# A two-layer attention and convolution kernel: the stage between the two, with its first loads, last softmax sums, interleaving and row normalisation rearranged

## The chip, the cores and the metric

The kernel runs on one core of one Trainium2 chip. The metric is the device time of one execution in microseconds, the median of three runs. The engines are named as in the profile: PE (TensorE, matrix products and transposes), PEld (its weight loads), DVE (VectorE), ACT (ScalarE), POOL (GpSimd) and SP (SyncE, which here only issues DMAs). Each engine executes its own instructions in program order and waits at an instruction until what it needs is there, so whatever stands behind a waiting instruction waits too.

## What is computed

`x` has 2048 rows of 640 numbers. Four blocks follow each other, each on the LayerNorm of the rows and added to `x`: attention (32 heads of 20), a long convolution, attention again, the convolution again, with the same weights.

```python
x = x + _A_ref(_layernorm(x), wqkv, wo)    # softmax(q k^T / sqrt(20)) v, then @ wo
x = x + _B_ref(_layernorm(x), ...)         # y = irfft(rfft(u) * rfft(K)) + u * D_skip
x = x + _A_ref(_layernorm(x), wqkv, wo)
x = x + _B_ref(_layernorm(x), ...)
# K[d, l] = 2 Re sum_n C[d, n] dt[d] exp(A[d, n] dt[d] l), 640 x 2048, the same in both layers
```

## The kernel before the change

**Attention.** The 32 heads are taken in eight groups of four, and each group in four blocks of 512 queries: 32 blocks, one after the other. For each block PE makes scores `S` (L866), ACT exponentiates them into `pt` (L869), and PE multiplies `pt` with the values into two accumulators `pa` (L900). One extra column of the values holds ones, so row 20 of each head's accumulator is the sum that its softmax divides by. At the end of a block (L903 to L950) DVE adds the two accumulators into `oc`. The sums then take a way through DRAM: POOL writes them out (`sums`, `dn<-oc`), reads them back spread over 128 partitions (`load`, `dr<-dn`), DVE inverts them (`invert`), POOL writes them (`back`, `dn<-dr`) and reads them back repeated for each row of a head (`spread`, `db<-dn`), and DVE multiplies (`scale`, `oc<-oc,db`). In the first layer `scale` waits in a list until the next block's accumulators have been emptied. POOL then stores `oc` to `ot` in DRAM (`store_block`). The second layer has another way for its last block only, `at_once` (L882): a 128 by 128 selector matrix `dsel` is multiplied with `oc`, which repeats the sums over the rows of their heads in one product `m<-oc,dsel`, and DVE clamps, inverts and multiplies.

**Between attention and convolution** (`out_proj`, L1310). For each of the 16 row tiles, `ot` is loaded (`otl`), split into a rounded part `oh` and a rest `ol`, and multiplied with `wo` in 30 products `po` of 320 columns (10 with `ol`, then 20 with `oh`). DVE adds the two results to `x` and takes the row statistics. When two row tiles are done, `ln` (L1660, `ln_u` at L1214) normalises both: a chain of small DVE operations with one ACT square root ends in `nb`, then ACT writes `u` and its rounding `uh` for each of the two, and POOL (DVE for the last row tile) the rest `ul`.

In the first layer this stage also transforms the convolution kernel `K` (`ktransform`, L1237). Its work is cut into 70 steps, and each step issues its own transposes or products and the copies that empty them: `by_time` (transposes `pkt<-kl`, copies `ktrh` on ACT and `ktrl` on DVE), `first_stage` (24 products `pkx`, copies `kx`), `turned` (transposes `pkt<-kx`, copies `kxt`) and `ends` (32 small products `pkf`, copies `kn`, stored as `kha` and `khb`). Steps and products share PE: after every eighth product `po` one step is issued (`weave(1)`, L1333), and what is left of the steps follows behind the last product (`weave(1000)`, L1366). The transforms' PSUM tiles come from the pool `X`, which has two buffers.

The first channel block of `K` is read into `kl` (`load_kl`, L1210). In the first layer this is issued on SP among other loads when the last attention block begins (`rest` in `prefetch`, L1181): three parts of `x`, then `skip`, `f2`, then `kl`. Before its transposes DVE adds one column to it (`kl<-kl,skip`, L1246).

**Convolution** (`ssm`, L1382). Five channel blocks of 128 run through a software pipeline of 55 turns (L1505). `stage1` makes products `psx` from `uh` and `ul`, which ACT and DVE empty into the two halves of `x1`; `stage2a` transposes (`pst`, emptied by ACT into `xt`); `sets` makes further products, `product` multiplies with the transformed kernel on DVE (shuffle `t`, `ka`) and POOL (`kb`, `ka`), and `stage3` and `stage4` transform back (`psv`, `psy`). All eight parts of `stage1` for channel block 0 come ahead of the pipeline (L1499); those of block 1 go one into each of its first eight turns, beside that turn's `pst`. Both use the pool `X`, but for parts 2, 3, 6 and 7 of block 0, which use the pool `M` (two buffers).

## Time and profile before

| | us |
|---|---|
| median of three runs | 2674.0 |
| the three runs | 2670.18, 2674.0, 2676.64 |
| the profiled execution, its own time | 2673.58 |
| its span, first to last instruction | 2671.8 |
| PE busy, ACT busy, DVE busy, POOL busy | 2496.7, 2344.9, 1510.4, 817.3 |
| first layer, end of the last attention product to the end of the last `po` | 1091.8 to 1259.6 |
| first layer, first `pst` of the convolution | 1283.7 |
| second layer, first `pst` of the convolution | 2527.7 |

All times within the execution are microseconds from the start of the span. A row of the timeline gives start, duration, engine, source line, operation, what is written and read with its shape, a count, and in brackets how long the engine sat idle before it and what ended that idle time. Nearly every DVE and ACT row has line 78, a helper that records the operations, so they are told apart by their tiles. A table of stretches gives, for each stretch, the busy time of each engine with the number of instructions, and the granted clock of PE as a share of full speed.

### The profile page before, as it was taken

How to read it: one execution, taken by the hardware profiler on the slowest of the kernel's cores; microseconds unless marked ns; L12 is line 12 of the kernel's file. 1: busy time of each engine (PE TensorE's matmuls, PEld its weight loads, DVE VectorE, ACT ScalarE, POOL GpSimd, SP SyncE). 2: the span in 40 equal slices, each digit the busy share in tenths (PEclk: the TensorE clock that was granted, in tenths of full speed). 3: DMA queues.
4: the chain of work that ended last, by engine and by line, in shares of the span. 5: the costliest groups of instructions: out<-in, count | busy, mean ns of one | idle time of the engine just before them, and what ended most of it. 6: DMA issues, size and time to landing. Idle time of an engine off the chain costs nothing.

```text
span 2671.8 us, 118793 instructions
## 1 busy us (share of the span) xinstructions
PE 2496.7 (93%) x52386; PEld 1412.8 (53%) x52386; DVE 1510.4 (57%) x3407; ACT 2344.9 (88%) x2763; POOL 817.3 (31%) x1250
## 2 busy tenths in 40 slices
PE   7899999999999988798898999999999998999898
PEld 3445444444444433587796444454444443444798
DVE  8687778778855884376787333231233221154775
ACT  7899999999999999555765799999999999999474
POOL 1123334233332423311581122222222222222285
PEclk9999999999999999899999999999999999999899
DMA  6523222222221222553652121121121113222366
GB/s 208 184 52 86 61 77 71 74 63 69 65 53 48 61 58 75 185 187 150 230 174 70 43 57 51 51 59 46 43 66 38 54 29 93 69 66 56 129 192 182
DMA packets 186446, 242.21 MB, mean 91 GB/s; under 512 B 43616, under 2 KB 128832, under 8 KB 184256
## 3 DMA queue, kind: packets, MB, share of 16 engines
q1 hardware_dynamic: 149904, 188.22, 22.2%
q0 software_dynamic: 36016, 46.30, 7.2%
q8 instruction: 413, 6.77, 1.0%
q14 instruction: 113, 0.93, 0.1%
HBM read 158.37 MB, written 76.01 MB: 88 GB/s over the span
## 4 chain that ended last, share of the span: by engine, by line
ACT 57%; PE 19%; issue 13%; DMA 5%; DVE 4%; POOL 1%; SPq 0%; ACTq 0%; POOLq 0%; DVEq 0%
ACT pt L78 54%; PE psy L1412 3%; PE psv L1412 2%; PE pa L900 2%; PE psx L1412 2%; PE po L193 2%; PE S L866 2%; PE pst L1433 1%; DMA kl<-kd 1%; DVE x L78 1%; PE pkt L196 1%; PE pq L771 1%; PE m L618 1%; DMA qop<-qs 1%; PE pkx L193 1%
## 5 line engine op out<-in xcount | busy, mean ns | idle before, releaser
L78 ACT ACTIVATE pt<-S 128x1024 f32<-128x1024 f32 x2048 | 1927.7, 1033 | 32.5 <-PE S L866 20.3
L900 PE MATMUL pa<-pt,V 64*32 64x512 f32 x16384 | 1094.4, 590 | 0.2 <-DVE oc L78 0.2
L866 PE MATMUL S<-qop,kop 61*32 61x512 f16 x16384 | 873.6, 381 | 86.5 <-ACT pt L78 67.7
L866 PEld LDWEIGHTS <-kop 61*32 61x32 f16 x16384 | 365.4, 89 | 740.3 <-issue 624.4
L900 PEld LDWEIGHTS pa<-pt,V 64*32 64x32 f32 x16384 | 311.9, 106 | 68.7 <-issue 7.9
L78 POOL DMA_DIRECT2D dn<-oc x252 | 124.0, 499 | 591.4 <-DVE oc L78 573.2
L78 DVE TENSOR_SCALAR qc<-m 128x512 f32<-128x512 f32 (+1 forms) x68 | 46.8, 688 | 282.7 <-PE m L618 282.7
L78 POOL DMA_DIRECT2D db<-dn x252 | 126.9, 510 | 139.0 <-DMA dn<-dr 136.1
L78 POOL DMA_DIRECT2D ot<-oc x256 | 130.1, 516 | 81.6 <-DVE oc L78 52.0
L78 DVE COPY oc<-pa 128x512 f32<-128x512 f32 x64 | 44.2, 691 | 194.3 <-PE pa L900 183.4
L618 PE MATMUL m<-xh,wh 64*32 64x512 f16 x2560 | 144.2, 378 | 2.9 <-DVE qc L78 2.9
L618 PE MATMUL m<-xh,wl 64*32 64x512 f16 x2560 | 143.8, 376 | 0.0
L618 PE MATMUL m<-xl,wh 64*32 64x512 f16 x2560 | 143.1, 376 | 0.0
L78 ACT COPY xt<-pst 128x1024 f16<-128x1024 f16 x80 | 81.2, 1015 | 59.7 <-PE pst L1433 59.7
L618 PEld LDWEIGHTS <-wh 64*32 64x32 f16 x5120 | 90.1, 93 | 76.5 <-issue 34.8
L78 POOL DMA_DIRECT2D dn<-dr x63 | 35.0, 555 | 304.9 <-DVE dr L78 289.8
L1461 POOL TENSOR_TENSOR kb<-t,kb 128x512 f32<-128x512 f32 x76 | 97.1, 1278 | 84.8 <-DVE t L78 46.0
L78 DVE TENSOR_SCALAR V<-m 128x160 f32<-128x160 f32 x64 | 20.7, 324 | 161.3 <-PE m L584 161.3
L78 DVE TENSOR_TENSOR kb<-ktab 128x512 f32<-128x512 f32 x160 | 106.3, 683 | 0.0
L584 PEld LDWEIGHTS <-xh 128*128 128x128 f16 x960 | 79.5, 98 | 44.8 <-issue 28.9
L335 PEld LDWEIGHTS m<-kb,ka 128*32 128x32 f32 x3840 | 61.2, 110 | 74.8 <-issue 56.4
L1461 POOL TENSOR_TENSOR ka<-ka,kb 128x512 f32<-128x512 f32 x76 | 97.4, 1281 | 6.0
(312 smaller groups left out, 3944.2 us busy)
## 6 DMA issues: line engine op xcount, KB each, us to landing
ka<-kha SPq DMA_DIRECT2D x80, 256.0 KB
kb<-khb SPq DMA_DIRECT2D x80, 256.0 KB
db<-dn POOLq DMA_DIRECT2D x252, 64.0 KB, 3.2
kop<-ks SPq DMA_DIRECT2D x176, 80.0 KB
kpw<-wd POOLq DMA_DIRECT2D x60, 192.0 KB, 4.6
qop<-qs SPq DMA_DIRECT2D x256, 40.0 KB
ot<-oc POOLq DMA_DIRECT2D x256, 40.0 KB, 2.8
kha<-kn SPq DMA_DIRECT2D x20, 512.0 KB
```

The costliest lines, as they stand in the source:

```text
L78: made = f(out, *a, **k)
L193: chain(te.matmul(*a, **k))
L196: chain(te.transpose(*a, **k))
L335: chain(te.matmul(ps[32 * j:32 * j + 32, c8, :], a[n][:, ch, :], b[n][:, dd, :], start=(n == 0), stop=(n == 2), tile_position=(0, 32 * j)))
L584: chain(te.matmul(ps[:, :n], a_[:, ct, sl], m[:, ct, :], start=(k == 0), stop=(k == 14)))
L618: chain(te.matmul(ps[r][32 * t:32 * t + 32, :], a_[rows, ct, 32 * u:32 * u + 32], m[rows, ct, 512 * v:512 * v + 512], start=(k == 0), stop ...
L771: te.matmul(pq, a_[:, ct, :], m[:, ct, sl], start=(n == 0), stop=(n == 14))
L866: chain(te.matmul(S[32 * t:32 * t + 32, 512 * r:512 * r + 512], kt_[rows, kc + 32 * t:kc + 32 * t + 32], qt[rows, :], start=True, stop=Tru ...
L900: chain(te.matmul(pa[r][32 * j:32 * j + 32, :], V[rows, kt, VP * h:VP * h + 32], pts[j // 2][rows, 512 * (j % 2):512 * (j % 2) + 512], sta ...
L1412: at("pe", te.matmul(*a, **k))
L1433: at("pe", te.transpose(pt[:, k, g, :], of_group(x1[k], 4 * q + g), id16))
L1461: at("pool", getattr(ge, f)(*a))
```

## The change

It has six parts.

1. In `prefetch` the small loads and `kl` are put ahead of the second to fourth part of `x`, and a selector `dsel` for the first layer (`late[0]`) is loaded with them. The addition `kl<-kl,skip` of block 0 is tied behind the DVE instruction that was last issued when turn 12 of the last attention block was written (`late[1]`).
2. The last block of the first layer takes the way `at_once`, as that of the second layer does.
3. One step of `ktransform` is issued ahead of the first product `po`, and then one after every seventh product instead of every eighth.
4. `ln` makes the statistics of a pair at once, as before, but the writing of `u`, `uh` and `ul` is a piece for each row tile, and after each row tile's products one piece is issued. This holds in both layers.
5. `stage1` of channel block 1 takes its PSUM tiles from `M` for parts 1, 3 and 5, in both layers.
6. `stage1` of channel block 0 takes all its tiles from `X` in the second layer; in the first it keeps `M` for parts 2, 3, 6 and 7.

```diff
--- before.py
+++ after.py
@@ -883,7 +883,7 @@
 
             pb = pst("M", [P, 512], F32, tag="m0", name="m0")
             db = ev.tile([P, 512], F32, bufs=1, name="db")
-            te.matmul(pb, dsel[0], oc, start=True, stop=True)
+            te.matmul(pb, (dsel or late)[0], oc, start=True, stop=True)
             ve.tensor_scalar_max(db, pb, 1e-30)
             ve.reciprocal(db, db)
             ve.tensor_mul(oc, oc, db)
@@ -912,7 +912,7 @@
                 sums_[0] = plan.dve + 0.15
                 while scaled:
                     scaled.pop(0)()
-                if dsel and blk == NBK - 1:
+                if blk == NBK - 1:
                     later.append((plan.dve, lambda: at_once(oc, blk)))
                     return
 
@@ -1125,6 +1125,8 @@
                             load_k(g, j, 1)
                         if g2 == g and qb2:
                             load_q(g, j, qb2, n + 1)
+                if kt == 12 and first_layer and n == len(turns) - 1:
+                    late.append(ve.last)
                 if kt == 8 and g2 != g:
                     need(NEED[g2])
                     for j in range(2):
@@ -1174,11 +1176,13 @@
                       w1.tile([P, 2, 32], F32, name="f2"), w1.tile([P, 4, NI // 2, 4, 32], F32, name="kx1"),
                       *(w1.tile([P, NI, P], F16, name=f"ktr{n}") for n in "hl"),
                       *(w1.tile([P, 4, 4, P], F32, name=f"kxt{n}") for n in range(2))]
+            late[:] = [w1.tile([P, P], F32, name="dsel")]
 
             def small():
                 sy.dma_start(kl0[1], dsk)
+                sy.dma_start(late[0], c_dn)
                 sy.dma_start(kl0[2], c_f2.rearrange("p (s m) -> p s m", s=2))
-            rest.extend((small, lambda: load_kl(0)))
+            rest[1:1] = small, lambda: load_kl(0)
             with tc.tile_pool(name="wos", bufs=NCT, side="right") as ws:
                 for ct in range(NCT):
                     wt = ws.tile([P, D], F32, name="wot")
@@ -1205,7 +1209,7 @@
             weights(ct)
         rest.extend(lambda ct=ct: halves(ct) for ct in range(NCT))
         return x, c, woh, wol, w2
-    ups, kl0 = [], []
+    ups, kl0, late = [], [], []
 
     def load_kl(b):
 
@@ -1243,7 +1247,7 @@
         def by_time(b, h):
 
             if h == 0:
-                ve.tensor_add(kl[:, 0:1], kl[:, 0:1], skip[:, b:b + 1])
+                tie(ve.tensor_add(kl[:, 0:1], kl[:, 0:1], skip[:, b:b + 1]), None if b else late[1])
             klv = kl.rearrange("d (p i) -> d i p", i=NI)
             for i4 in (2 * h, 2 * h + 1):
                 pt = pst("X", [P, 4, P], F32, tag="X", name="pkt")
@@ -1329,8 +1333,9 @@
                 return
             matmul(*a, **k)
             many[0] += 1
-            if many[0] % 8 == 0:
+            if many[0] % 7 == 0:
                 weave(1)
+        weave(1)
         to_come = {s: 0 for s in range(NI)}
         for s, c0, c1 in rows.left + [e[0] for e in rows.loaded + first]:
             to_come[s] += 1
@@ -1353,16 +1358,16 @@
                 load()
                 load = None
             if due:
-                ln(*due.pop(0))
+                due.pop(0)()
             if not to_come[s]:
                 if s >= NI - LG or s % LG and s - 1 in whole:
-                    due.append((s, 1))
+                    due.extend(ln(s, 1))
                 elif s % LG == LG - 1:
-                    due.append((s + 1 - LG, LG))
+                    due.extend(ln(s + 1 - LG, LG))
             if due and len(whole) == 0:
-                ln(*due.pop(0))
+                due.pop(0)()
         while due:
-            ln(*due.pop(0))
+            due.pop(0)()
         weave(1000)
 
     def ssm_consts(c):
@@ -1415,7 +1420,8 @@
 
             def stage1(b, x1, i2):
                 bs = slice(b * P, b * P + P)
-                pool, tag = ("X", "X") if b or i2 % 4 < 2 else ("M", "mm")
+                spare = b == 1 and i2 in (1, 3, 5) or not b and i2 % 4 > 1 and not last
+                pool, tag = ("M", "mm") if spare else ("X", "X")
                 ps = pst(pool, [P, 2, 2, P], F32, tag=tag, name="psx1")
                 for i in range(2):
                     s = 2 * i2 + i
@@ -1658,10 +1664,18 @@
                     up2 = c2.enter_context(tc.tile_pool(name="up2", bufs=2 + n))
 
                     def ln(i0, m):
-                        ln_u(x, i0, m, ln_stats(lambda i: x[:, i0 + i, :], m), uh, ul, up2, not general)
+                        held = []
+
+                        def one(i):
+                            if not held:
+                                held.extend(ln_stats(lambda i: x[:, i0 + i, :], m))
+                            mv, rs = held
+                            ln_u(x, i0 + i, 1, (mv[:, i:i + 1, :], rs[:, i:i + 1]), uh, ul, up2, not general)
+                        return [lambda i=i: one(i) for i in range(m)]
                     if general:
                         for i0 in range(0, NI, LG):
-                            ln(i0, LG)
+                            for f in ln(i0, LG):
+                                f()
                     else:
                         if n == 0:
                             filler[:] = ktransform(consts[0]), 0.0, False
```

Three places show what this does to the order of instructions. The first is the start of the first layer's `out_proj`. On DVE before the change, from the addition to `kl` on (`dr` are the sums of the last block but one, `pa` the accumulators of the last block, and the multiplication with `db` is that of the last block but one):

```order
L78 TENSOR_TENSOR kl<-kl,skip 128x1
L78 TENSOR_SCALAR dr<-dr 128x16
L78 RECIPROCAL dr<-dr 128x16
L78 CAST oh<-otl 128x640
L78 TENSOR_TENSOR ol<-otl,oh 128x640
L78 COPY oc<-pa_25900 128x512
L78 TENSOR_TENSOR oc<-oc,pa_25901 128x512
L78 TENSOR_TENSOR oc<-oc,db 128x512
L78 SCALAR_TENSOR_TENSOR ktrl<-pkt,ksc,ktrh 128x512
L78 TENSOR_TENSOR ol<-otl,oh 128x640
L78 SCALAR_TENSOR_TENSOR ktrl<-pkt,ksc,ktrh 128x512 x2
```

After the change, DVE at the same place, from the end of the first row tile's split on (`m` is the product with `dsel`):

```order
L78 TENSOR_TENSOR ol<-otl,oh 128x640
L78 TENSOR_TENSOR kl<-kl,skip 128x1
L78 COPY oc<-pa_25901 128x512
L78 TENSOR_TENSOR oc<-oc,pa_25902 128x512
L78 TENSOR_TENSOR oc<-oc,db 128x512
L78 SCALAR_TENSOR_TENSOR ktrl<-pkt,ksc,ktrh 128x512
L78 TENSOR_SCALAR db<-m_26437 128x512
L78 SCALAR_TENSOR_TENSOR ktrl<-pkt,ksc,ktrh 128x512
L78 RECIPROCAL db<-db 128x512
L78 TENSOR_TENSOR ol<-otl,oh 128x640
L78 TENSOR_TENSOR oc<-oc,db 128x512
L78 SCALAR_TENSOR_TENSOR ktrl<-pkt,ksc,ktrh 128x512 x2
```

The addition now stands behind the inversion of `dr` and the first split, of which only the last row is shown, and the last block's own inversion, of 512 columns, stands between the second and the third `ktrl`. On PE, the same place before and after, from the last attention product on:

```order
L900 MATMUL pa_25901<-pt,V_93 32x512 x4
L193 MATMUL po<-woh,ol 128x320 x8
L196 MATMUL pkt<-ident,kl 128x128 x8
L193 MATMUL po<-woh,ol 128x320 x2
L193 MATMUL po<-woh,oh 128x320
L193 MATMUL po<-wol,oh 128x320
L193 MATMUL po<-woh,oh 128x320
```

```order
L900 MATMUL pa_25902<-pt,V_93 32x512 x4
L196 MATMUL pkt<-ident,kl 128x128 x8
L886 MATMUL m_26437<-oc,dsel 128x512
L193 MATMUL po<-woh,ol 128x320 x7
L196 MATMUL pkt<-ident,kl 128x128 x8
L193 MATMUL po<-woh,ol 128x320 x3
L193 MATMUL po<-woh,oh 128x320
L193 MATMUL po<-wol,oh 128x320
L193 MATMUL po<-woh,oh 128x320
```

Eight transposes and the product with `dsel` now stand ahead of the first `po`.

The second place is ACT in the same stage, at the third pair of row tiles (`lt` is the square root). Before:

```order
L78 CAST oh<-otl 128x640
L78 ACTIVATE ktrh<-pkt,ksc 128x512
L78 ACTIVATE lt<-va 128x2
L78 ACTIVATE ktrh<-pkt,ksc 128x512
L78 COPY kn_27343<-pkf_27324 128x512
L78 ACTIVATE u<-x,nb,rs 128x640 x2
L78 CAST uh<-u 128x640 x2
L78 COPY kn_27347<-pkf_27326 128x512
```

After:

```order
L78 ACTIVATE kxt_25870<-pkt,ksc 128x512
L78 ACTIVATE lt<-va 128x2
L78 ACTIVATE ktrh<-pkt,ksc 128x512
L78 ACTIVATE u<-x,nb,rs 128x640
L78 ACTIVATE ktrh<-pkt,ksc 128x512
L78 CAST uh<-u 128x640
L78 ACTIVATE u<-x,nb,rs 128x640
L78 COPY kn_27436<-pkf_27417 128x512
L78 CAST uh<-u 128x640
L78 COPY kn_27440<-pkf_27419 128x512
```

A pair was four operations in a row and is now taken apart by the transform's copies. Of the seven pairs, three come apart like this; in the others three of the four operations still stand together, or all four (the first pair).

The third place is DVE in the second layer between the last products `po` and the first `pst`: the small operations of the last row tile (`va` to `nb`), among the eight `x<-psx` that empty `stage1` of block 0. Before:

```order
L78 RECIPROCAL rs<-lt 128x1
L78 TENSOR_TENSOR x_55462<-psx_55493,x_55461 128x4x4x32
L78 TENSOR_TENSOR lt<-rs 128x1
L78 TENSOR_TENSOR x_55462<-psx_55508,x_55461 128x4x4x32
L78 TENSOR_TENSOR lt<-lt,va 128x1
L78 TENSOR_TENSOR x_55462<-psx_55523,x_55461 128x4x4x32
L78 TENSOR_SCALAR lt<-lt 128x1
L78 TENSOR_TENSOR x_55462<-psx_55538,x_55461 128x4x4x32
L78 TENSOR_TENSOR rs<-rs,lt 128x1
L78 TENSOR_TENSOR x_55462<-psx_55553,x_55461 128x4x4x32
L78 SCALAR_TENSOR_TENSOR nb<-mv,rs 128x1
L78 TENSOR_TENSOR ulx<-u,uhx 128x640
```

After:

```order
L78 TENSOR_SCALAR va<-mv 128x1
L78 TENSOR_TENSOR x_55476<-psx_55492,x_55475 128x4x4x32
L78 RECIPROCAL rs<-lt 128x1
L78 TENSOR_TENSOR lt<-rs 128x1
L78 TENSOR_TENSOR lt<-lt,va 128x1
L78 TENSOR_SCALAR lt<-lt 128x1
L78 TENSOR_TENSOR x_55476<-psx_55507,x_55475 128x4x4x32
L78 TENSOR_TENSOR rs<-rs,lt 128x1
L78 SCALAR_TENSOR_TENSOR nb<-mv,rs 128x1
L78 TENSOR_TENSOR x_55476<-psx_55522,x_55475 128x4x4x32
L78 TENSOR_TENSOR x_55476<-psx_55537,x_55475 128x4x4x32
L78 TENSOR_TENSOR ulx<-u,uhx 128x640
```

Seven of the eight `x<-psx` stood ahead of `nb`, two of them above these rows; now three do, one of them above.

## The prediction, made before the changed kernel ran

> **What bounds the kernel now.** First the page: in which of 40 slices PE and ACT are busy, in tenths.
>
> ```profile
> PE   7899999999999988798898999999999998999898
> ACT  7899999999999999555765799999999999999474
> ```
>
> In the attention both stand at 9. Of those parts only the last block of the first layer is touched, so they should stay as they are. ACT falls to 5 to 7 in slices 17 to 22, between the first attention and the second: that is the stage which the change rearranges. I read it in stretches next (busy time of PE, PEld, DVE, ACT and POOL, then the granted clock), together with the places where either convolution starts.
>
> ```profile
> 1091.80:1106.36 14.56, 5.05 (x25) 4.78 (x25) 4.47 (x10) 2.10 (x3) 4.92 (x10) 0.72 0.60 194
> 1091.80:1259.60 167.80, 148.69 (x1610) 126.53 (x1611) 112.39 (x248) 84.97 (x139) 32.43 (x38) 0.94 0.47 166
> 1259.60:1283.70 24.10, 19.95 (x330) 14.61 (x327) 17.21 (x34) 14.74 (x26) 0.00 (x0) 1.00 0.56 220
> 1283.70:1292.70 9.00, 5.78 (x80) 5.07 (x81) 2.74 (x4) 5.65 (x8) 0.00 (x0) 1.00 0.85 296
> 2512.80:2527.70 14.90, 7.39 (x74) 6.81 (x72) 9.90 (x26) 7.65 (x13) 3.14 (x3) 0.68 0.09 16
> ```
>
> PE sets the pace: it is busy 148.69 of the 167.80 us up to the last `po`, DVE two thirds of them, ACT half. The change can win only what PE now waits for, and the stretches name five such places: 9.5 us idle at the start (5.05 busy of 14.56), smaller waits up to 1259.6, the steps left over behind the last `po`, the first turns of the convolution, and in the second layer half of the 14.9 us ahead of the first `pst`.
>
> **Step a, the start.** The long waits there, and how long the small DMAs took to land (last number of a DMA row):
>
> ```profile
> 1082.19 0.59 POOL L78 DMA_DIRECT2D dr<-dn  x1 [3.74 <-DMA dn<-oc]
> 1091.82 0.16 DVE L78 TENSOR_TENSOR kl<-kl,skip 128x1 f32<-128x1 f32 x1 [27.07 <-DMA kl<-kd]
> 1104.95 0.69 DVE L78 TENSOR_TENSOR oc<-oc,db 128x512 f32<-128x512 f32 x1 [9.89 <-DMA dn<-oc]
> 1106.36 1.12 PE L196 MATMUL pkt<-ident,kl 128*128 128x128 f32 x4 [7.44 <-DVE ktrl L78]
> 1110.87 0.33 PE L193 MATMUL pkx<-ktrh,e1s 128*128 128x128 f16 x1
> dr<-dn POOLq DMA_DIRECT2D x1, 8.0 KB, 5.1
> dn<-dr POOLq DMA_DIRECT2D x1, 8.0 KB, 1.7
> db<-dn POOLq DMA_DIRECT2D x4, 64.0 KB, 8.3
> db<-dn POOLq DMA_DIRECT2D x4, 64.0 KB, 2.1
> ```
>
> DVE sat 27.07 us before the addition to `kl`, because `kl` is loaded behind three parts of `x`. Behind the addition stands the inversion of the last block but one, so the sums came back as `db` only at 1104.95. The first `ktrl` is behind that multiplication, and PE, out of transform buffers, idled 7.44 us. After the change the inversion is ahead of the addition. `dr<-dn`, issued at 1082.19, takes 5.1, so `dr` is there at 1087.3. Half a microsecond for the inversion, 1.7 for `dn<-dr` and some 2.5 for four issues put the last `db` load at 1092. It lands after 2.1 (the landing with quiet queues) to 8.3 (beside the 2 MB load of `e1s`, as before): between 1094 and 1100. The load of `e1s` waits for attention's memory, free at 1091.8, and so will run beside `db`: I take 1100, 5 us earlier than before.
>
> What DVE does then is longer, since the new way of the last block stands between the second and the third `ktrl`:
>
> ```profile
> L886 PE MATMUL m<-oc,dsel x2: 592/644/697, 2469.3 to 2469.9; 128*128 128x512 f32 x2
> L78 DVE RECIPROCAL db<-db x1: 3346/3346/3346, 2473.3 to 2473.3; 128x512 f32<-128x512 f32 x1
> 1105.56 0.75 DVE L78 SCALAR_TENSOR_TENSOR ktrl<-pkt,ksc,ktrh 128x512 f16<-128x512 f32 x1
> 1106.22 0.82 DVE L78 TENSOR_TENSOR ol<-otl,oh 128x640 fp32r<-128x640 f32 x1
> 1154.49 1.23 PE po L193 x8
> ```
>
> From `db` on: 0.69 multiplication, 0.75 `ktrl`, a clamp of the same 512 columns at 0.69, 0.75 `ktrl`, 3.35 inversion, 0.82 `ol`, 0.69 multiplication, 0.75 the third `ktrl`. That is 8.5 us until the first `pkx` has a buffer: 1108.5 with `db` at 1100, where it was 1110.87. But by then PE will have done 14 `po` instead of 26, and 12 at 0.15 are 1.8 us still to come. **Gain 0.6.** With `db` at 1095 it is 5.6, with `db` at 1103 a loss of 2.4. The product with `dsel` (1.24 us) falls into PE's wait, and would be paid if that wait went. The DRAM way of the last block, now gone, is no term: its rows are needed only from row tile 12 on. Nor are the parts of `x` that load later: row tile 4 comes some 17 steps on.
>
> **Step b, up to the last `po`.** Whom PE waited for from 1112 to 1259.6 (total, times, longest), one such place on ACT, and the stretches of PE behind the two longest waits:
>
> ```profile
> PE pkx L193 <- ACT kx L78: 4.3, 3, 2.1
> PE pkt L196 <- ACT kxt L78: 3.4, 2, 2.6
> 1220.54 1.73 ACT L78 ACTIVATE u<-x,nb,rs 128x640 f32<-128x640 f32 x2 [1.28 <-DVE nb L78]
> 1222.18 1.33 ACT L78 CAST uh<-u 128x640 f16<-128x640 f32 x2
> 1224.05:1229.00 4.95, 4.95 (x45) 4.75 (x45) 1.67 (x3) 1.01 (x2) 1.67 (x2) 0.66 0.07 21
> 1248.03:1252.10 4.07, 3.98 (x16) 3.42 (x16) 2.26 (x4) 1.38 (x2) 0.60 (x1) 0.58 0.58 227
> ```
>
> ACT is the one waited for, 7.7 us. It waits 1.28 for the statistics, the pair then keeps it 3.1, and PE's next buffer is emptied only behind that. After the two longest waits, 2.1 and 2.6 us, the granted clock is 0.66 for 4.95 us and 0.58 for 4.07, which costs 1.7 each. Together 11.1 us hang on this. Three of seven pairs come apart into singles of 1.55 us, three more lose a part of their block: I take half, 5.5. Against it, one product less between two steps is 0.15 us less cover for each of 69 steps; if one step in ten is short of cover, by some 0.15 or a little more, that is 1 us. **Gain 4.5**, between 0 (the wait for `nb` decides, not the length of the block) and 11.1.
>
> The Trainium skill bears on the clock ("TensorE: Matmul & The Clock Gate", Part 1): PE falls to half clock after about 3.4 us of idling, so that shorter waits should leave it warm. By that rule a wait removed here would give back only itself, and step b would be 2.9 us. The trace differs: waits of 2.1 and 2.6 us are followed by clocks of 0.66 and 0.58, and I go by the rows.
>
> **Step c, behind the last `po`.** There are 70 steps and 480 products. By eights, 59 steps stand ahead of the last product and 11 run behind it (the sixtieth comes just after it); now 69 stand ahead and one behind. What a step costs PE where it runs dense, and the end of the last row tile's chain:
>
> ```profile
> 1254.62 1.35 PE pkx L193 x24
> 1230.26 0.90 PE pkt L196 x8
> 1257.20 1.07 PE pkf L193 x32
> 1264.90 0.82 DVE L78 TENSOR_TENSOR ul<-u,uh 128x640 f16<-128x640 f32 x1
> 1279.39 4.97 DVE L78 TENSOR_TENSOR x<-psx,x 128x512 f16<-128x512 f32 x8 [0.50 <-ACT x L78]
> ```
>
> Three `pkx` steps, four `pkt` and three `pkf` move ahead of the last `po`: 3 x 1.35 + 4 x 0.90 + 3 x 1.07 = 10.9 us. Behind it the last row tile's chain is then bare. It took 6.1 us from the last `po` to the end of `ul` at 1265.72, hidden until now beside the steps, and the eight `x<-psx` on DVE take 4.97, seven of them behind `ul`. With the two `kn` copies that now stand in the chain at 0.7 each, 12 us. So 22.9 instead of 24.1: **gain 1.2**, between -2 and 4.
>
> **Step d, the first turns in both layers.** Two waits of PE, ACT's two operations in a turn, and POOL's first product, all in the first layer:
>
> ```profile
> 1289.53 0.22 PE L1412 MATMUL psx<-uh,e1s 128*128 128x128 f16 x1 [0.88 <-DVE x L78]
> 1285.94 0.59 ACT L78 CAST x<-psx 128x512 f16<-128x512 f32 x1
> 1286.79 1.01 ACT L78 COPY xt<-pst 128x1024 f16<-128x1024 f16 x1 [0.26 <-PE pst L1433]
> 1295.06 1.28 POOL L1461 TENSOR_TENSOR kb<-t,kb 128x512 f32<-128x512 f32 x1 [37.03 <-DMA ka<-kha]
> ```
>
> A turn takes 2.25 us (9.0 for the four from 1283.7 on), and each `psx` waits for DVE to empty the one before, since `pst` and `psx` alternate on two buffers. With every other `psx` in `M` this falls away, and ACT's 1.01 and 0.59 set a turn: 9.0 shrink to about 7.5, with a first turn as before. POOL then runs without a break, so what it starts earlier stays won. **Gain 1.5 in each layer**, and 0.4 more in the first, where POOL's first product waited last for a load that now goes out earlier in this sequence: 3.4, between 0 and 5.
>
> **Step e, second layer, ahead of the first `pst`.** The third `psx`, the first and the last `x<-psx`, and the end of the last row tile's chain:
>
> ```profile
> 2516.17 0.27 PE L1412 MATMUL psx<-uhx,e1s 128*128 128x128 f16 x1 [3.34 <-DVE x L78]
> 2517.24 0.69 DVE L78 TENSOR_TENSOR x<-psx,x 128x512 f16<-128x512 f32 x1 [0.35 <-ACT x L78]
> 2525.45 0.82 DVE L78 TENSOR_TENSOR ulx<-u,uhx 128x640 f16<-128x640 f32 x1 [1.80 <-ACT uhx L78]
> 2527.67 0.69 DVE L78 TENSOR_TENSOR x<-psx,x 128x512 f16<-128x512 f32 x1 [1.40 <-ACT x L78]
> ```
>
> With all parts in `X`, the third `psx` waits for the first `x<-psx`, which ends at 2517.93: 1.7 later than now. But four `x<-psx` fewer stand ahead of `nb`, so `ulx` ends some 2.4 us sooner, near 2523.9. The two buffers are then passed on every 1.6 us, and the last `x<-psx` ends near 2526.8, not 2528.36. **Gain 1.6**, between -1.5 and 2.5.
>
> **The sum.** 0.6 + 4.5 + 1.2 + 3.4 + 1.6 = 11.3. The profiled execution took 2673.58, 0.4 below the median of 2674.0, so 2662.3, rounded to **2662**.
>
> **The rivals.** *Entries only* (2666.8): ACT's wait for `nb` holds PE as long as before, and b gives nothing; the others leave 6.8. For it: ACT waited 1.28 for `nb` ahead of that pair. Against it: the pair's 3.1 us are longer than that wait. *All waits go* (2649.8): a 5.6, b 11.1, c 2, d 3.4, e 1.6, together 23.7. Against it: half of the pairs still block ACT. *Cover too thin* (2685): not PE but the emptying of buffers sets a step, so that each keeps its 167.8 / 59 = 2.84 us. Then 69 steps take 196 and 12 follow, 208 where it was 191.9: 16.1 slower, less 5.0 for d and e, 11.1. From 2.68 us a step on the kernel is slower than before; my forecast is (167.8 + 10.9 - 5.1) / 69 = 2.52. For it: PE does wait for copies. Against it: DVE is busy 67% and ACT 51% of the stretch. *The earlier load does not help* (2665): `db` lands at 1103 after all, beside `e1s`, and step a alone turns to -2.4.
>
> **How the numbers follow.** About 0.2%, 5.3 us, is what a measurement of this kernel can tell from no change, so faster means below 2668.7. Forecast 0.5 (2656 to 2666, the late load within it), entries only 0.24 (2666 to 2671, two thirds of it faster), all waits go 0.14 (2646 to 2656), nothing to tell to 2679 0.05, cover too thin 0.07. Faster is 0.5 + 0.14 + 0.16 = 0.80, slower 0.07, the rest, 0.13, the same. The range from 2650 to 2671 leaves out 0.12 above and 0.05 below.
>
> **What would show it.** Step a: `oc<-oc,db` near 1100 and the first `pkx` near 1108.5. Step b: the last `po` 173.6 us behind the last attention product, PE's waits for ACT halved. Step c: the first `pst` 12 us behind the last `po`. Step d: turns of 1.6 to 2 us. Step e: `ulx` ending 11 us behind the last `po`. If a step takes over 2.7 us, I am wrong altogether.

## The result and the profile after

The changed kernel took 2667.03 us (median of 9 runs, 2664.5 to 2668.55), the kernel before 2674.97 beside it (9 runs, 2670.18 to 2680.11). The ratio is 0.9969, 95% interval 0.9959 to 0.9979: faster by 0.3%, some 8 us where 11.3 to 12 were forecast. The profiled execution took 2665.94 (span 2664.1) against 2673.58 (span 2671.8).

First the same two rows of the 40 slices, of the changed kernel:

```profile
PE   7899999999999998799898999999999998999898
ACT  7899999999999999565765799999999999999474
```

ACT still falls to 5 to 7 between the attentions. Next the same five stretches (busy time of PE, PEld, DVE, ACT and POOL, granted clock, DMA share, GB/s). The first attention ends at 1093.18 here, 1.39 us later than in the profile before, ahead of all that was changed, so places are compared by their distance from that end:

```profile
1093.18:1105.02 11.84, 3.24 (x18) 2.31 (x18) 2.79 (x5) 1.89 (x3) 2.45 (x5) 0.86 0.75 237
1093.18:1270.68 177.50, 158.31 (x1818) 132.10 (x1823) 123.14 (x263) 91.80 (x152) 27.05 (x27) 0.96 0.49 172
1270.68:1282.57 11.89, 8.66 (x129) 6.90 (x129) 8.85 (x22) 7.34 (x14) 0.00 (x0) 0.86 0.74 265
1282.57:1289.87 7.30, 5.55 (x80) 5.17 (x81) 2.75 (x4) 5.47 (x8) 0.00 (x0) 1.00 0.98 348
2509.52:2522.70 13.18, 6.40 (x73) 5.55 (x73) 10.10 (x26) 7.44 (x13) 2.91 (x3) 0.87 0.10 21
```

The last three are as forecast: 11.9 us from the last `po` to the first `pst` (forecast 12), 7.3 for the first four turns (7.5), 13.2 in the second layer (13.3; the experiments come back to this one). The second is not: the last `po` ends 177.5 us behind attention, where 173.6 were forecast. So the missing time lies between the end of attention and the last `po`, steps a and b. The start, on DVE and then on PE, and how long two small DMAs took (last number of their rows):

```profile
1087.80 0.17 DVE L78 TENSOR_SCALAR dr<-dr 128x16 f32<-128x16 f32 x1 [20.21 <-DMA dr<-dn]
...
1103.61 0.69 DVE L78 TENSOR_TENSOR oc<-oc,db 128x512 f32<-128x512 f32 x1 [8.93 <-DMA db<-dn]
...
1106.14 3.34 DVE L78 RECIPROCAL db<-db 128x512 f32<-128x512 f32 x1
```

```profile
1105.02 1.12 PE L196 MATMUL pkt<-ident,kl 128*128 128x128 f32 x4 [8.14 <-DVE ktrl L78]
...
1111.56 0.22 PE L193 MATMUL pkx<-ktrh,e1s 128*128 128x128 f16 x1 [2.57 <-DVE ktrl L78]
```

```profile
db<-dn POOLq DMA_DIRECT2D x4, 64.0 KB, 7.6
dn<-dr POOLq DMA_DIRECT2D x1, 8.0 KB, 5.9
```

The inversion of `dr` is where the forecast had it, at 1087.8. But `dn<-dr` then took 5.9 us, not 1.7, and `db` 7.6. The three parts of `x` are now issued behind `kl`, from 1078.1 on, and still under way: between the issue of `dn<-dr` and that of `db` the DMA engines are full (share 1.11, 368 GB/s), where the profile before has a share of 0.02 at the same step. So DVE, which executes in order, got to the multiplication only at 1103.61, 10.4 us behind attention (before 13.2, forecast 8.2). PE waited 8.14 us and, behind the inversion of 512 columns, 2.57 more. And whom PE waited for from there to the last `po` (total, times, longest), with DVE's and PE's rows at the longest new wait:

```profile
PE pkt L196 <- ACT kxt L78: 3.5, 2, 2.3
PE po L193 <- DVE x L78: 3.4, 3, 2.9
PE pkf L193 <- ACT kxt L78: 0.4, 1, 0.4
PE pkx L193 <- ACT kx L78: 0.4, 1, 0.4
```

```profile
1209.47 0.16 DVE L78 TENSOR_TENSOR kl<-kl,skip 128x1 f32<-128x1 f32 x1 [3.87 <-DMA kl<-kd]
1209.55 0.48 DVE L78 TENSOR_TENSOR x<-x,po 128x320 f32<-128x320 f32 x1
```

```profile
1210.08 0.70 PE L193 MATMUL po<-woh,ol 128*128 128x320 f32 x3 [2.93 <-DVE x L78]
```

The waits for ACT did halve, from 8.4 us to 4.3. In their place stands one for DVE: the change holds only the first addition to `kl`. The additions of later blocks are placed freely, and in this order one stands ahead of `x<-x,po` while its load is still on the way. DVE sits 3.87 us, the `po` buffers are not emptied, PE waits 2.93.

### The profile page after: what moved, and what is told of

It is laid out like the page before. It is cut to its first block, busy times and chain, and to the rows that moved or that the text cites. A ratio compares the mean times of both kernels' runs of the same rounds, so it can differ in the third digit from the quotient of the medians.

```text
span 2664.1 us, 118804 instructions
## 1 busy us (share of the span) xinstructions
PE 2492.7 (94%) x52388; PEld 1408.8 (53%) x52388; DVE 1517.5 (57%) x3417; ACT 2342.6 (88%) x2763; POOL 813.9 (31%) x1240
## 4 chain that ended last, share of the span: by engine, by line
ACT 58%; PE 19%; issue 10%; DVE 4%; DMA 4%; POOL 1%; SPq 0%; ACTq 0%; POOLq 0%; DVEq 0%
ACT pt L78 56%; PE psy L1417 3%; PE psv L1417 2%; PE pa L900 2%; PE po L193 2%; PE psx L1417 2%; PE S L866 1%; PE pst L1439 1%; PE pkx L193 1%; PE pkt L196 1%; PE m L618 1%; PE pq L771 1%; DVE x L78 1%; PE pkf L193 1%; DMA kl<-kd 0%
```

## The experiments

The theory after reading the two traces: c, d and e are as forecast. Step a fell short because `db` landed late and DVE's order passes that on to PE. In step b singles are worth at least what was forecast, but a later addition to `kl` takes part of it back. Rivals: the last part carries the whole gain, singles are worth nothing, the closer steps cost cover, or it is chance which steps meet which rows' work.

All times in one table: the median, the ratio to the runs of the kernel before on the same chip (medians of 2673.1 to 2675.9), and from the one profiled execution of each the distances from the end of attention (A) to the first `pkx`, to the last `po`, from there to the first `pst`, and from A to the last `psy` of the first layer.

| kernel | us | ratio (95%) | A to `pkx` | A to last `po` | to `pst` | A to last `psy` |
|---|---|---|---|---|---|---|
| before | 2674.97 | 1 | 19.1 | 167.9 | 24.1 | 328.9 |
| changed | 2667.03 | 0.9969 (0.9959 to 0.9979) | 18.4 | 177.5 | 11.9 | 324.1 |
| pools_only | 2670.6 | 0.9987 (0.9976 to 0.9999) | 18.7 | 170.2 | 24.1 | 333.6 |
| early_only | 2672.76 | 0.9993 (0.9981 to 1.0005) | 15.8 | 166.3 | 24.1 | 327.5 |
| lead_only | 2678.43 | 1.0009 (0.9999 to 1.0019) | 19.2 | 178.0 | 23.1 | 337.8 |
| pairs_back | 2675.28 | 1.0001 (0.9993 to 1.001) | 18.1 | 187.1 | 12.3 | 335.0 |
| every8 | 2674.4 | 0.9998 (0.9988 to 1.0009) | 18.1 | 174.1 | 23.1 | 333.6 |
| pairs8 | 2680.82 | 1.0024 (1.0013 to 1.0035) | 18.2 | 174.4 | 23.1 | 333.9 |
| phase7 | 2668.96 | 0.9973 (0.9963 to 0.9984) | 18.1 | 181.0 | 12.0 | 327.6 |
| hold_kl | 2663.79 | 0.9963 (0.9949 to 0.9977) | 18.1 | 175.1 | 10.6 | 320.7 |
| bounce | 2662.57 | 0.9953 (0.9937 to 0.9969) | 15.1 | 174.1 | 10.7 | 319.5 |
| pool_scale | 2658.55 | 0.9946 (0.9933 to 0.9959) | 10.1 | 170.2 | 10.6 | 315.6 |
| hold_pool | 2653.9 | 0.9917 (0.9898 to 0.9937) | 10.2 | 166.5 | 11.9 | 313.0 |
| hold_bounce_pool | 2659.06 | 0.9937 (0.9919 to 0.9956) | 9.8 | 173.0 | 12.1 | 319.7 |

How finely the distances can be read: pools_only has the instructions of the kernel before up to the last `po`, and its last `po` still comes 2.4 us later. So a distance of one execution holds to 2 or 3 us; the medians carry the verdicts, the rows the reasons.

### Two parts alone: pools_only and early_only

In the kernel before, only the buffers of `stage1`:

```diff
-                pool, tag = ("X", "X") if b or i2 % 4 < 2 else ("M", "mm")
+                spare = b == 1 and i2 in (1, 3, 5) or not b and i2 % 4 > 1 and not last
+                pool, tag = ("M", "mm") if spare else ("X", "X")
```

> The kernel before with only the last part of the change: the PSUM buffers of the convolution's first products. Theory (d and e are as forecast, read from the two traces): the first turns of each layer are 1.7 to 2 us shorter and the stretch between the last po and the first pst of the second layer 1.4 to 1.7, so 5 to 6 us faster than before, 2668.5 to 2670. Rival 1 (this part carries the whole gain, the rest nets nothing): 8 us faster, 2667. Rival 2 (what the turns win is given back by the chain behind them): 2674.

Measured: 2670.6, 4.7 us by the medians, 0.3 to 6.4 by the interval, so rival 1 falls. The first four turns take 7.3 us in the first layer and 7.28 in the second, where kernels with the old buffers take 9.0 to 9.6 and 9.3: d is this part, as the theory has it.

Step e is not. The second layer's stretch ahead of the first `pst` is 13.6 us here, which looks like the forecast beside the 14.9 of the profile before. But early_only and lead_only, below, keep the old buffers and the old order on DVE at this place, and their stretches are:

```profile
2509.62:2523.03 13.41, 5.85 (x73) 5.43 (x72) 9.61 (x26) 7.66 (x13) 3.11 (x3) 0.86 0.05 10
2523.20:2536.90 13.70, 6.13 (x73) 5.71 (x71) 9.71 (x26) 7.56 (x13) 3.12 (x3) 0.88 0.05 11
```

They take 13.4 and 13.7 us at a granted clock of 0.86 and 0.88, where the profile before has 0.68. All kernels with the new buffers take 13.2 to 13.8. `ulx` does end sooner with them (11.4 us behind the last `po` here, 12.2 and 12.5 in these two), but the first `pst` gains a few tenths at most. The 1.7 us between the profiles before and after are mostly the low clock of one execution.

In the first layer this execution (2677.7 us, well above the median) gave its turns back. POOL's first product there:

```profile
1300.22 1.27 POOL L1462 TENSOR_TENSOR kb<-t,kb 128x512 f32<-128x512 f32 x1 [37.52 <-DMA ka<-kha]
```

It starts 4.5 us behind the first of the products `psx<-xt` (before 2.4, changed kernel 2.0), and the page names a load of the transformed kernel as what it waited for. (The page says `ka`; the product reads `kb`, whose load was issued right behind, and DVE had used its `ka` at 1298.11, so `kb` is likelier.) The last transform blocks are stored late while eleven steps stand behind the last `po`, so SP's first load of `ka` goes out 6.6 us ahead of `psx<-xt`, where the changed kernel has 10.8. The same holds in every profile with the new buffers: POOL starts 3.9 to 4.5 us behind with a step per 8 products (pools_only, every8, pairs8), and 2.0 behind with a step per 7 (the changed kernel, pairs_back, phase7). So in the first layer the shorter turns need the earlier steps to pay in full: two parts of the change that the forecast had added up as independent.

In the kernel before, only the order of the loads and the held addition:

```diff
-            rest.extend((small, lambda: load_kl(0)))
+            rest[1:1] = small, lambda: load_kl(0)
...
-                ve.tensor_add(kl[:, 0:1], kl[:, 0:1], skip[:, b:b + 1])
+                tie(ve.tensor_add(kl[:, 0:1], kl[:, 0:1], skip[:, b:b + 1]), None if b else late[0])
...
+                if kt == 12 and first_layer and n == len(turns) - 1:
+                    late.append(ve.last)
```

> The kernel before with part 1 alone: the first block of kl loaded ahead of the rows and its addition held; no lead step, no inversion by a product, pairs at 8, old buffers. Theory (the inversion of the last block but one is no longer behind the addition, but db still lands late, beside e1s): the multiplication by db 2.5 to 3 us sooner after attention than before (13.2), the first pkx 2.5 to 4 us sooner than 19.1, and 2670 to 2673. Rival (the early load wins nothing, since the queues hold db up all the same): 2673.5 to 2676.

Measured: 2672.76, 3.1 us by the medians, with an interval that takes in no change. DVE's row of the multiplication, with attention's end at 1090.68:

```profile
1100.86 0.69 DVE L78 TENSOR_TENSOR oc<-oc,db 128x512 f32<-128x512 f32 x1 [8.68 <-DMA dn<-oc]
```

10.2 us behind attention instead of 13.2, and the first `pkx` 3.3 sooner, with as many `po` done as before. The theory holds for the place; for the time the measurement is not fine enough alone.

### Singles and spacing: pairs_back, every8, pairs8

The changed kernel with pairs again, with a step per 8 products again (the lead step stays), and with both:

```diff
-                        held = []
-...
-                        return [lambda i=i: one(i) for i in range(m)]
+                        return [lambda: ln_u(x, i0, m, ln_stats(lambda i: x[:, i0 + i, :], m), uh, ul, up2, not general)]
```

```diff
-            if many[0] % 7 == 0:
+            if many[0] % 8 == 0:
```

> The changed kernel with rows normalised in pairs again, all else kept. Theory (singles free ACT, and their worth is the halved wait of PE for ACT): PE waits for ACT 3 to 5 us longer, the last po is 3 to 6 us later, 2670 to 2673. Rival (it was the denser steps or the earlier load that halved the waits, singles are worth nothing): 2666 to 2668.

> The changed kernel with a step per 8 products again (the step ahead of the first product stays), all else kept, rows still singly. Theory (steps that stand closer pay only because they leave none behind the last po, and they cost little cover): nine or ten steps move behind the last po again, so the last po comes 8 to 11 us sooner after attention than the 177.5 us of the changed kernel and the first pst stands 20 to 23 us behind it instead of 11.9; together 0 to 3 us slower, 2667 to 2670. Rival (closer steps cost cover, 0.15 us for most of 69 steps): 3 to 6 us faster than the changed kernel, 2661 to 2664.

> The changed kernel with rows in pairs and a step per 8 products again. Theory (the two parts hang together: the block of a pair costs little where steps stand 8 products apart, as in the kernel before, and 8 to 10 us where they stand 7 apart): 2667 to 2671, that is 4 to 8 us faster than pairs at 7. Rival (pairs cost 8 to 10 us at any distance, and the distance nothing): 2674 to 2677. Second rival (singles pay at neither distance): the same as singles at 8.

Measured, as ratios to the kernel before:

| | a step per 7 | a step per 8 |
|---|---|---|
| singles | 0.9969 | 0.9998 |
| pairs | 1.0001 | 1.0024 |

At 7, singles are worth 0.0032, about 8.5 us: undoing them alone takes the whole gain. The last `po` of pairs_back comes 9.6 us later in the profiles. Its waits of PE up to the last `po` (of the 3.0 us in the last row, 2.2 lie ahead of the first `pkx`), and the stretch from the first `pkx` on:

```profile
PE po L193 <- DVE x L78: 3.8, 3, 3.1
PE pkt L196 <- ACT kx L78: 3.8, 2, 1.9
PE pkt L196 <- ACT kxt L78: 3.5, 2, 2.3
PE pkx L193 <- DVE ktrl L78: 3.0, 2, 2.2
```

```profile
1110.11:1279.08 168.97, 156.71 (x1786) 131.71 (x1791) 112.91 (x246) 88.88 (x147) 22.26 (x18) 0.94 0.44 157
```

PE does the same 1786 instructions as in the changed kernel in 156.7 us instead of 151.3, at a clock of 0.94 instead of 0.98, and stands idle 12.3 instead of 7.8. In these two executions half of what the singles are worth is wait, and half is the lower clock. The theory had the direction and half the size.

The spacing was mis-judged outright. Steps at 8 were expected to cost 0 to 3 us; they cost 0.0029, about 7.8. The rival (closer steps cost cover) falls further still, since it expected the opposite sign. Two reasons in the trace of every8. Its waits up to the last `po` are longer than at 7, not shorter, and ACT's rows at the longest show why:

```profile
PE pkt L196 <- ACT kxt L78: 5.4, 3, 2.7
PE pkx L193 <- ACT kx L78: 4.4, 2, 3.0
```

```profile
1190.33 1.73 ACT L78 ACTIVATE u<-x,nb,rs 128x640 f32<-128x640 f32 x2 [1.28 <-DVE nb L78]
1191.97 0.71 ACT L78 CAST uh<-u 128x640 f16<-128x640 f32 x1
1192.58 0.57 ACT L78 COPY kx<-pkx 128x512 f32<-128x512 f32 x1
```

At this spacing both singles of a pair, though written as two, come between the same two copies of the transform: the order puts `u` twice and `uh` ahead of the `kx` that PE waits for. And behind the last `po` the convolution starts late again. POOL's first product, and SP's first load of `ka`, with the first `psx<-xt` at 1299.36:

```profile
1303.23 1.29 POOL L1467 TENSOR_TENSOR kb<-t,kb 128x512 f32<-128x512 f32 x1 [36.72 <-DVE x L78]
```

```profile
1292.66 0.43 SPq L78 DMA_DIRECT2D ka<-kha  x1
```

3.9 us behind it where the changed kernel has 2.0, with the loads out only 6.7 us ahead. The page puts the wait down to DVE, which had written `t` at 1301.18; a load fits better, but is inferred. The theory of pairs8 falls likewise: expected 2667 to 2671, measured 2680.8. Singles and spacing do not hang together as the theory said; they nearly add (singles are worth 0.0032 at 7, 0.0026 at 8).

### The additions held: hold_kl

```diff
-skip[:, b:b + 1]), None if b else late[1])
+skip[:, b:b + 1]), late[-1])
...
-                        ve.tensor_scalar_mul(xt[:, q], pt, ksc[:, 1:2])
+                        made = ve.tensor_scalar_mul(xt[:, q], pt, ksc[:, 1:2])
+                        if not (t or h):
+                            late.append(made.ins)
```

> The changed kernel with the later additions to kl held, too: each stands behind the first kxt product of its own block. Theory (b fell short because an addition that waits for its load stands ahead of x<-x,po on DVE): DVE's wait of 3.87 us at 1209 goes, with it PE's 2.9 us and most of the 1.7 us that the lower clock cost behind it: 3 to 5 us faster than the changed kernel, 2662 to 2664. Rival (kl is late for its transposes anyway, so that PE waits a little later for pkt): 2666 to 2668.

Measured: 2663.79, 3.2 us below the changed kernel by the medians and 1.6 by the ratios, whose intervals overlap, so the time alone does not show a gain. DVE no longer waits for `kl` there, and in the waits of PE `po` for DVE is down to 0.5. The theory holds for the wait, not for the clock: a low clock returned behind another wait. PE's row and the 4 us behind that wait in hold_kl, and then, of the changed kernel, the 4 us behind the wait that is gone now and the 4 us behind the same 2.27 us wait:

```profile
1232.81 1.66 PE L196 MATMUL pkt<-ident,kl 128*128 128x128 f32 x8 [2.27 <-ACT kxt L78]
```

```profile
1232.81:1236.81 4.00, 4.00 (x31) 3.40 (x47) 1.90 (x3) 2.10 (x3) 1.09 (x1) 0.57 0.23 89
```

```profile
1210.08:1214.08 4.00, 4.00 (x40) 2.15 (x41) 3.53 (x14) 1.30 (x3) 0.00 (x0) 0.60 0.09 33
1239.42:1243.42 4.00, 4.00 (x52) 2.97 (x53) 2.52 (x5) 2.56 (x5) 1.10 (x1) 1.00 0.23 89
```

The clock of 0.60 behind the wait of 2.93 us is gone, but the same 2.27 us are now followed by 0.57, where the changed kernel has 1.00. In both kernels PE was busy for 5.73 of the 8 us that end with this wait, at a clock of 1.00. So neither the length of this wait nor the amount of work ahead of it tells what the clock does next.

### The start: bounce and pool_scale

The changed kernel with the last block of the first layer by way of DRAM again:

```diff
-            te.matmul(pb, (dsel or late)[0], oc, start=True, stop=True)
+            te.matmul(pb, dsel[0], oc, start=True, stop=True)
...
-                if blk == NBK - 1:
+                if dsel and blk == NBK - 1:
```

> The changed kernel with the last block of the first layer inverted by way of DRAM again. Theory (of step a: the inversion of 512 columns, 3.34 us, and its clamp stand ahead of the third ktrl while PE waits for it): the first pkx comes 3 to 4.5 us sooner, 14 to 15.5 us after attention instead of 18.4, and 2662.5 to 2665. Rival (the DRAM way makes DVE wait later, at the multiplication by the second db, or row tiles 12 to 15 come late): 2667 to 2672.

Measured: 2662.57, 4.5 us below the changed kernel by the medians (the intervals just overlap), with the first `pkx` 15.1 us behind attention, 3.3 sooner than in the changed kernel. DVE's row of the first two `ktrl`, PE's of the transposes behind them:

```profile
1103.41 1.40 DVE L78 SCALAR_TENSOR_TENSOR ktrl<-pkt,ksc,ktrh 128x512 f16<-128x512 f32 x2
```

```profile
1104.21 1.97 PE L196 MATMUL pkt<-ident,kl 128*128 128x128 f32 x8 [9.29 <-DVE ktrl L78]
```

The theory holds for the place: there the inversion of 512 columns, 3.34 us, takes back what the early load wins (3.3 in early_only). The wait ahead of `ktrl` is as long as ever.

The changed kernel with that multiplication on POOL, and with a free tile of the transform for the last block's inversion, so that it doesn't wait for `db`'s buffer either:

```diff
-                    ve.tensor_mul(oc, oc, db[0])
+                    (ge if first_layer and blk == NBK - 2 else ve).tensor_mul(oc, oc, db[0])
...
-            db = ev.tile([P, 512], F32, bufs=1, name="db")
+            db = ev.tile([P, 512], F32, bufs=1, name="db") if dsel else kl0[6][:, 0].rearrange("p g k -> p (g k)")
```

> The changed kernel with the multiplication of the last block but one by db on POOL instead of DVE, and a buffer of its own for the last block's inversion, so that the first ktrl no longer stands behind a wait for db. Theory (a fell short because db landed late, at 1103.5, and DVE's order made PE wait for it): the first ktrl at about 1098, the first pkx at 1106 instead of 1111.6, 4 to 6 us faster, 2661 to 2663. Rival (the load of e1s, or PE's lack of other work, takes the place of that wait): within 1.5 us of the changed kernel, 2665.5 to 2667.

Measured: 2658.55, 8.5 us below the changed kernel by the medians (6.2 by the ratios, whose intervals just touch), more than expected. The first `ktrl` runs at 1095.36, 2.8 us behind attention, and PE's only long wait in the start is now the one ahead of the first `pkx`:

```profile
1102.71 0.27 PE L193 MATMUL pkx<-ktrh,e1s 128*128 128x128 f16 x1 [3.48 <-DVE ktrl L78]
```

It comes 10.1 us behind attention, 8.3 sooner than in the changed kernel, where 5.6 were expected. This shows what was left of step a: with `kl` loaded early, the start is bound by the multiplication by a late `db` that stands ahead of `ktrl` on DVE. (Whether moving it would have paid without the early load was not run.)

### Alignment: lead_only and phase7

The kernel before with one step ahead of the first product, and the changed kernel with its steps 3 products earlier:

```diff
                 weave(1)
+        weave(1)
```

```diff
-        due, many = [], [0]
+        due, many = [], [3]
```

> The kernel before with one edit: a first step ahead of the first product, so that every step meets the rows' own work 8 products sooner. Theory (what b is worth hangs on which steps meet which rows' work on ACT and DVE; pairs at 8 with the lead step had 13.7 us of waits up to the last po where the kernel before has 8.8): the stretch from the first pkx to the last po gets 4 to 7 us longer, though it holds only one step more, 2676 to 2680. Rival (the lead step only saves what stood behind the last po, and it was the early load and the last block's inversion that cost pairs8 its time): 2672 to 2674.

> The changed kernel with the same steps at the same distance, only shifted: after products 4, 11, 18 and so on instead of 7, 14, 21. Theory (alignment of steps and rows sets the waits): PE's waits up to the last po differ from the 7.7 us of the changed kernel by 2 us or more, and the time by 2 to 6 us either way, outside 2665 to 2669. Rival (the distance and the singles set them, not the alignment): 2665.5 to 2668.5.

Measured: lead_only 2678.43, ratio 1.0009, interval 0.9999 to 1.0019. PE's waits from the first `pkx` to the last `po`, and that stretch:

```profile
PE pkt L196 <- ACT kxt L78: 5.9, 3, 2.6
PE pkx L193 <- ACT kx L78: 4.4, 3, 2.1
PE po L193 <- DVE x L78: 1.3, 4, 0.5
```

```profile
1112.55:1271.32 158.77, 145.76 (x1604) 123.44 (x1604) 106.49 (x237) 82.45 (x135) 25.34 (x24) 0.95 0.45 162
```

13.0 us idle where the kernel before had 9.2 in its 148.8, at a clock of 0.95 instead of 0.97. The step alone, meant to save time, makes every later step meet the rows 8 products sooner, and this stretch is 10 us longer, of which 8 products and one step more of work are some 2.5 us. But this was the slowest of its twelve runs: by the medians the kernel is 2.6 us slower, and the interval just reaches no change. phase7 came out at 2668.96 with 9.2 us idle instead of 7.8: within the rival's waits, half a microsecond above its time. So it is not shown that alignment matters: at 8 with pairs the time hints at it, at 7 with singles nothing does.

### Together: hold_pool and hold_bounce_pool

> The changed kernel with both edits: all additions to kl held, and the multiplication by db on POOL. Theory (two waits at different places, so the gains add, but for the 1.25 us behind the last po that both showed): from the end of attention to the last psy of the first layer 311.5 to 314 us, where the changed kernel takes 324.1; 2654.5 to 2657. Rival (one gain is given back where the other removes a wait): 2658 to 2660.

> The changed kernel with three edits: all additions to kl held, the multiplication by db of the last block but one on POOL, and the last block by way of DRAM again. Theory (with db out of DVE's way the 3.34 us inversion is what PE still waits for, 3.5 us ahead of the first pkx, but e1s lands only about 9 us after attention): the first pkx 9 to 9.7 us after attention instead of 10.2, and 0.5 to 1.5 us faster than without the way by DRAM, 2652 to 2653.5. Rival 1 (the whole 3.5 us come back): 2650. Rival 2 (the multiplication of the last block now waits on DVE for its own db): 2655 or more.

Measured: hold_pool, both edits, 2653.9, ratio 0.9917 (0.9898 to 0.9937), the best of all, some 13 us below the changed kernel, with an interval well apart from its. By the medians the gains add (3.2 and 8.5). With the way by DRAM as a third edit it is 2659.06, 5 us worse by the medians, though the intervals overlap: rival 2 is right in kind. PE's row at the first `pkx` of hold_pool, then DVE's and PE's of hold_bounce_pool:

```profile
1104.05 0.23 PE L193 MATMUL pkx<-ktrh,e1s 128*128 128x128 f16 x1 [3.57 <-DMA e1s<-in_c_e]
```

```profile
1108.73 0.17 DVE L78 TENSOR_SCALAR dr<-dr 128x16 f32<-128x16 f32 x1 [9.59 <-DMA dr<-dn]
```

```profile
1109.79 0.27 PE L193 MATMUL pkx<-ktrh,e1s 128*128 128x128 f16 x1 [4.21 <-DVE kx L78]
```

In hold_pool PE waits for the load of `e1s`, so the last block's inversion, which ends earlier, costs next to nothing any more (without it the first `pkx` comes 9.8 us behind attention instead of 10.2). By way of DRAM DVE sits 9.59 us in front of the last block's own `dr` (the rival had named its `db`), with the emptying of `pkx` behind it, and PE waits 4.21. The inversion by a product, which costs 3.3 us at the start of the changed kernel, is by these rows the better way as soon as DVE's other wait is gone.

## Why the prediction was right, and where it was off

Faster was forecast and measured, and 2667.0 lies within 2650 to 2671. The likeliest time was 5 us too low. Measured in the two profiles, with the forecast behind: a -0.8 (0.6), b 2.0 (4.5), c 1.3 (1.2), d 4.1 (3.4), e 1.7 (1.6); together 8.3 (11.3). (The spans differ by 7.7: attention ended 1.4 us later in the profile after, and the rest was 0.8 shorter.) That the sum came so near is in part luck: step e matches only by the low clock of the profile before. With e at a few tenths, a, b and e are each short by 1 to 2.5 us, and d is 0.7 above.

- **Step a** failed at `dn<-dr`: "1.7" for its landing was that of the profile before, when the parts of `x` were through. Issued earlier it ran beside them and took 5.9, and the multiplication by `db` came 10.4 us behind attention. Forecast were 8.2 (`db` at 1100); the rival "the earlier load does not help" had 11.2 (`db` at 1103), so the rival was nearer. The 3.35 us for the last block's inversion were right (bounce: 3.3). The count of products was not: 24 `po`, not "26", stand ahead of the first `pkx` before, so 10 were still to come and not 12, and the forecast's own gain should have read 0.9.
- **Step b** is the term that was mis-sized, as far as distances good to 2 or 3 us can tell. Halved waits for ACT were right (8.4 to 4.3). Singles were sized too low: "I take half, 5.5" against 8.5 in pairs_back. The counter-term, "one product less between two steps is 0.15 us less cover", had the wrong sign: closer steps were worth 7.8 us in all (every8). What was not in the sum at all is a later addition to `kl`, which the change does not hold: it made PE wait 2.93 us, with a clock of 0.60 for the 4 us behind. What that cost in time hold_kl does not settle (1.6 to 3.2 us, within the noise), and whether the lead step's shift of all steps took more is not shown (lead_only, phase7).
- **Cover too thin** was ruled out with 2.57 us a step (177.5 / 69) where 2.52 was forecast and 2.68 would have decided.
- **Step c** was right as a stretch, 11.9 for 12, but it is worth more than it says: with the steps out of the way the transform's last blocks are stored sooner, and the transformed kernel is there when POOL wants it. Only so could d keep its whole share in the first layer; pools_only lost it there.
- **Step d** was right in place and size: the four turns take 7.2 to 7.3 us in both layers of every kernel with the new buffers, but for the first layer of pairs_back (8.2).
- **Step e** had its number right by luck. It measured its gain against a row at a clock of 0.68, and kernels with the old buffers and a clock of 0.86 to 0.88 come within about half a microsecond of the changed one. `ulx` ended 11 us behind the last `po`, as forecast, but that moved the first `pst` by tenths.
- **The clock.** The prediction went by the rows, low clock behind waits of 2.1 and 2.6 us. The changed kernel bears them out: 0.60 behind a wait of 2.93. The Trainium skill ("TensorE: Matmul & The Clock Gate", Part 1) has PE fall to half clock after about 3.4 us of idling; these traces differ, with clocks of 0.57 to 0.66 behind waits of 2.1 to 2.9 us. But the rows are no rule either, as hold_kl shows: 2.27 us are followed by 0.57 there and by 1.00 in the changed kernel.

What stays open: what brings the low clock, how much of step b's shortfall is real, and whether the parts together cost more at 8 than alone. The ratios of pools_only, early_only and lead_only with the 0.0016 of the inversion would put pairs8 at 1.0005; it took 1.0024. The intervals of the five together are about 0.003 wide to either side, so this may be noise.

## What to carry to other kernels

When a load is moved forward, time every small DMA behind it with the traffic of its new place, not of its old one. On an engine that executes in order, look for every instruction that waits on a DMA, and ask what stands behind it: moving the multiplication by a late `db` to POOL and holding the additions to `kl` won another 13 us on top of the change's 8, without doing less work. Parts that touch one stage are not a sum; here shorter turns need earlier stores, and an inversion that costs 3.3 us in one order looks like the better choice in another. And before a gain is booked against a stretch of one profile, look at its granted clock, and at the same stretch in a second profile of the same code.

## What the runs showed of the hardware

A write of 8 KB to DRAM (`dn<-dr`) that landed in 1.7 us in the profile before, at a DMA share of 0.02, took 5.9 issued earlier, at a share of 1.11. The granted clock was 0.60 and 0.57 for 4 us behind waits of 2.93 and 2.27 us, and 1.00 behind another of 2.27, though PE had done the same work in the 8 us up to both. The same instructions took 2.4 us longer in one execution than in another up to the last `po` (pools_only and the kernel before), and a stretch of the second layer took 14.9 us at a clock of 0.68 in one and 13.4 at 0.86 in another (the kernel before and early_only).
